# Loading the second chunk's last two units as 32x32 squares and transposing them on VectorE, in an HGRN2 and SwiGLU kernel

## The chip, the cores and the metric

The kernel runs on one core of a Trainium2 chip. The metric is device microseconds of one execution. The time before is the median of three runs; one more execution was recorded by the hardware profiler, and all times inside the kernel come from it.

## The reference

Four batches of eight heads, a sequence of 768 positions and a head size of 48 go through a gated linear attention. Its output is brought into 3072 rows of 384 features, which a SwiGLU feed-forward block (384 to 1536 to 384) takes.

```python
B, H, S, D = 4, 8, 768, 48
f = 1.0 / (1.0 + np.exp(-f_logit))
state = np.zeros((B, H, D, D))
for t in range(S):
    state = f[:, :, t, :, None] * state + einsum('bhd,bhe->bhde', k[:, :, t], v[:, :, t])
    y[:, :, t] = einsum('bhd,bhde->bhe', q[:, :, t], state)

x = y.transpose(0, 2, 1, 3).reshape(B * S, H * D)
g = x @ w_gate
out = (g * sigmoid(g) * (x @ w_val)) @ w_out
```

All inputs and the output are fp32.

## The kernel before

**Units and chunks.** The sequence is cut into six chunks of 128 positions. A unit is one chunk of one batch, numbered u = 4c + b, so that chunk 0 holds units 0 to 3, chunk 1 units 4 to 7, and so on. `attention(u)` is a generator that emits one unit in small steps. The feed-forward block works on a whole chunk of all four batches (512 rows) at a time, one chunk behind the attention. Chunk 0's feed-forward is `mlp_plain`: gate and value products (L786) and twelve down steps `downs_abreast` (L809). Chunks 1 to 5 use `mlp_fifteen`, a scheme with fifteen half-size products in place of eighteen (L988), made possible by sums of weights and of tokens that VectorE forms (L889, L892, L895), and seven down products in place of eight (L1087, L1150).

**What a unit does.** The gate logits f go through a sigmoid. f, k and q must stand with the features on partitions (head pairs, 48 of 64 rows each). Two scans along the positions give the running products of the gates (L601 into `tail`, L627 into `gate`). k is multiplied by one and q by the other (L559). The scores k q (`sc`, L647) are masked on VectorE (L662, tile `A`), the output y is formed from the masked scores and v, and from q and the decayed state (L683, L687 or L708), and the state is updated (`dS` L728, L737). `kt` (L651, L660) is k turned back for dS. The outputs go to `xT`, the input of the feed-forward block: for batches 0 to 2 through a copy `yT` and ten small DMAs each (L698), for batch 3 directly (L723). Batch 3 needs the decayed state laid out as a block diagonal for that (`diagonal`, L567 to L570); it uses the same one-buffer ring, tag "x", as `yT`.

**Two ways to turn f, k and q.** For chunks 0 and 1 (`c < SQUARES`, with SQUARES = 2) each of f, k and q is loaded by one DMA into one of two raw buffers (L444), in pieces of 48 values (192 bytes), and transposed by four TensorE transposes each (tiles fTp, kTp and qTp, L575). The sigmoid is taken while fTp leaves PSUM (L586), except for unit 4, whose sigmoid is taken ahead. For chunks 2 to 5 each is loaded by four DMAs (L440), in pieces of four positions of 48 values (768 bytes), into a tile of squares (`rooms`, one each for f, k and q, made by `make_rooms` when the first part's memory is given back). The sigmoid is taken in place (L580), and VectorE transposes 32x32 blocks (f: L589, k: L597, q: L631).

**What sets the order.** The kernel has two parts. In the second, from the load of unit 8 on, each engine's order is the order of emission; blocks of the feed-forward stage and steps of the attention are merged by a table of due times (`SCORES`, `CHAINS`, `times`), in units of the feed-forward's own nominal microseconds, where 0 is the start of a chunk's fifteen-product stage. The list `sigmoid` in `times` has the due time of each unit's sigmoid. In the first part `take_turns` emits the feed-forward pieces of chunk 0 and the attention steps of chunk 1 in proportion, and a scheduler of the framework may place an instruction earlier or later on its engine than it was emitted, when the operands of another are ready first. The attention steps of a unit come in four groups of 3, 6, 3 and 3 yields (`parts`), sorted so that group s of batch b has rank 2b + s. The sums of weights are emitted in pairs between the down steps and tied by `behind` to follow the VectorE instruction emitted last. Around units 6 and 7 the emission is: down step 0, scores of unit 6, down step 1, fTp of unit 7, down steps 2 and 3, y and dS of unit 6, down step 4, kTp and qTp of unit 7 with its scans and products, down step 5, scores of unit 7, down steps 6 and 7, y and dS of unit 7, down steps 8 to 11.

**Loads in the first part.** `load_after(u)` is called at the end of a unit's products. For units 4 and 5 it loads units 6 and 7, two units ahead, into the raw buffer that has come free.

**The end.** `judge` takes the least gate product of all units. Were it below 2^-60, a general path would run instead; a branch on it stands at the very end. A branch hint for all engines is given in the last stage.

The functions that the change touches:

Of the kernel before, what the change touches and what calls it, by code (L numbers as in the profile page):

```python
# [9 lines left out]
FP32 = mybir.dt.float32  # L10
# [280 lines left out]
def short_path(ctx, tc, ident, least, judge, q, k, v, f_logit, moe_w_gate, moe_w_val, moe_w_out, out):  # L291
# [9 lines left out]
    nc = tc.nc  # L301
    B, H, S, D = q.shape
    C = 128
    NCH = S // C
    HP = H // 2
    W = 64
# [6 lines left out]
    NRAW = 2  # L313
    NROT = 2
    NV = 4
    SQUARES = 2
# [3 lines left out]
    att = ctx.enter_context(tc.tile_pool(name="att", bufs=1))  # L320
# [5 lines left out]
    first_pool = early.enter_context(tc.tile_pool(name="first", bufs=1))  # L326
# [9 lines left out]
                            pattern=[[1, C]], channel_multiplier=-1)  # L336


    raw = {nm: [first_pool.tile([128, H, W], FP32, tag=f"{nm}raw{i}", name=f"{nm}raw{i}") for i in range(NRAW)]
           for nm in "qkf"}  # L340
    for nm in "fkq":
        for t in raw[nm]:
            nc.gpsimd.memset(t[:, :, D:W], 60.0 if nm == "f" else 0.0)
# [20 lines left out]
    def pairs(t, off=0):  # L364
        return t[:, off:off + HP * N1].rearrange("p (a t) -> p a t", t=N1)
# [23 lines left out]
    units = [(b, c) for c in range(NCH) for b in range(B)]  # L389
# [5 lines left out]
    Q = 32  # L395
    NI = C // Q
    RUN = NI * D

    rooms = {}

    def make_rooms(pool):
        for nm in "fkq":
# [22 lines left out]
    def load(u, what="fkqv"):  # L425
        b, c = units[u]
        rows = slice(c * C, (c + 1) * C)
        inputs = dict(f=f_logit, k=k, q=q, v=v)
        for nm in "fkqv" if c < SQUARES else "fqkv":
            src = inputs[nm]  # L430
            if nm not in what:
                continue
            if nm == "v":
                dst = v_of(u)
            elif c < SQUARES:
                dst = raw[nm][u % NRAW]
            else:
                for n in range(4):
                    at = Q * (1 - n % 2)
                    nc.sync.dma_start(  # L440
                        out=rooms[nm][Q * n:Q * (n + 1), at:at + HP * RUN].rearrange("t (a e) -> t a e", a=HP),
                        in_=src[b, n // 2::2, rows, :].rearrange("a (t i) d -> t a (i d)", i=NI))
                continue
            nc.sync.dma_start(out=dst[:, :, 0:D], in_=src[b, :, rows, :].rearrange("h t d -> t h d"))  # L444
# [100 lines left out]
    def attention(u):  # L545
        b, c = units[u]
# [2 lines left out]
        gate, tail = (x[u % NROT if c < SQUARES else 0] for x in (gates, tails))  # L549

        diagonal = None

        def multiply(out, x, by):

            if c >= SQUARES:
                for_each = "p a (t j i) -> p a t j i"
                out, by = (t.rearrange(for_each, j=2, i=NI // 2) for t in (out, by))
                x = x.rearrange("p (j a t i) -> p a t j i", j=2, a=HP, i=NI // 2)
            nc.vector.tensor_tensor(out, x, by, ALU.mult)  # L559

        def decay():
            nonlocal diagonal
            if c:
                nc.vector.tensor_tensor(decayed[:, :, 0:D], states[b], whole.broadcast_to((128, HP, D)), ALU.mult)
            if c and b == B - 1:

                diagonal = att.tile([128, HP, 2 * D], FP32, tag="x", name="diagonal")  # L567
                nc.scalar.copy(diagonal.rearrange("p a d -> p (a d)"), spare.broadcast_to((128, HP * 2 * D)))
                for par in range(2):
                    nc.scalar.copy(diagonal[rows_of(par), :, par * D:(par + 1) * D], decayed[rows_of(par), :, 0:D])  # L570

        def transposed(name, src):
            p = bank(name)
            for a in range(HP):
                nc.tensor.transpose(p[:, a * C:(a + 1) * C],  # L575
                                    src[:, 2 * a:2 * a + 2, :].rearrange("t r d -> t (r d)"), ident)
            return p.rearrange("p (a t) -> p a t", t=C)

        if c >= SQUARES:
            nc.scalar.activation(squares("f"), squares("f"), AF.Sigmoid)  # L580
            if b == (c > SQUARES):

                nc.scalar.activation(spare, spare, AF.Silu)
        else:
            p = transposed("fTp", fr)
            nc.scalar.activation(pairs(gate)[:, :, 1:N1], p, AF.Copy if u in ahead else AF.Sigmoid)  # L586
        yield
        if c >= SQUARES:
            nc.vector.transpose(in_turn(pairs(gate)[:, :, 1:N1]), squares("f"))  # L589
        yield  # L590

        kT = att.tile([128, HP, C], FP32, tag="kT", name="kT")
        qT = att.tile([128, HP, C], FP32, tag="qT", name="qT", bufs=2)
        kp, qp = kT, qT
        if c >= SQUARES:
            kp = qT.rearrange("p a t -> p (a t)")
            nc.vector.transpose(parted(kp), split_squares("k"))  # L597
        yield

        n = HP * N1  # L600
        nc.vector.tensor_tensor_scan(tail[:, 0:n][:, ::-1], gate[:, 0:n][:, ::-1], floor[:, ::-1], 1.0,  # L601
                                     op0=ALU.mult, op1=ALU.max)
        whole = pairs(tail)[:, :, 1:2]
        nc.vector.reciprocal(pairs(start)[:, :, 0:1], whole)
        yield
        if c < SQUARES:
            kp = transposed("kTp", kr)
            qp = transposed("qTp", qr)
        multiply(kT, kp, pairs(tail, 2)[:, :, 0:C])
        yield  # L610
        turned = SQUARES < c < NCH - 1
# [8 lines left out]
                                  in_=beside[Q * r:Q * (r + 1)].rearrange("t i (a e) -> t (i a) e", e=Q))  # L620
        yield

        if c >= SQUARES:

            nc.scalar.copy(least[:, u, :], whole.rearrange("p a t -> p (a t)"))
            whole = least[:, u, :].unsqueeze(2)
        nc.vector.tensor_tensor_scan(gate[:, 0:n], gate[:, 0:n], start, 1.0, op0=ALU.mult, op1=ALU.add)  # L627
        yield
        if c >= SQUARES:
            qp = tail[:, 0:HP * C]  # L630
            nc.vector.transpose(parted(qp), split_squares("q"))  # L631
            load_after(u)
        yield
        multiply(qT, qp, pairs(gate)[:, :, 1:N1])
        nc.gpsimd.memset(pairs(gate)[:, :, 0:1], 0.0)  # L635
        if 0 < c < SQUARES:
            load_after(u)
        if c < SQUARES:
            decay()
        yield  # L640
# [9 lines left out]
            for a in range(HP):  # L650
                nc.tensor.transpose(p[:, a * C:(a + 1) * C], kT[:, a, :], ident)  # L651
        yield
        if c < SQUARES:
            nc.scalar.copy(least[:, u, :], whole.rearrange("p a t -> p (a t)"))
        if c < NCH - 1:
            kt = att.tile([128, HP * C], FP32, tag="kt", name="kt")
# [82 lines left out]

    def load_after(u):  # L740

        w = u + (1 if units[u][1] >= SQUARES else 2)
        if w < len(units) and (units[w][1] >= SQUARES) == (w == u + 1):
            load(w, "fkqv" if units[w][1] < SQUARES or w == SQUARES * B else "fkq")

    def attention_steps(c):

        runs = [attention(c * B + b) for b in range(B)]
        parts = [3, 6, 3, 3]
        order = sorted((2 * b + s, b, n) for b in range(B) for s, n in enumerate(parts))  # L750
        return [lambda b=b, n=n: [next(runs[b]) for _ in range(n)] for _, b, n in order]

    traced = nc.cur_bb.bb.instructions
# [16 lines left out]
    TH = TB // 2  # L770
# [98 lines left out]
    def times(c):  # L869
        at = [t for t, _ in SCORES[c]]  # L870
        outputs = [*at[1:], down[10] if c + 1 in SCORES and SCORES[c + 1][0][0] < -1 else LAST]
        sigmoid = [-14 if c == 3 else SCORES[c - 1][-1][0] - whole - 0.01 if c > 3 else 0, -4 if c == 3 else at[0] - 0.01, *[t - 0.01 for t in at[1:]]]
        masks = {"b": 2, "o": 0.9, "A": 1.5}
        return [[f, *steps, s + 0.02, s + masks[kind], s + 2.2, o, o + 0.01, o + 2.1]
                for f, steps, (s, kind), o in zip(sigmoid, CHAINS[c], SCORES[c], outputs)]
# [404 lines left out]


    mark = traced[-1]
    waiting = []
    for c in range(2, NCH):
        for b in range(B):
# [34 lines left out]
@with_exitstack  # L1320
def kernel(
    ctx: ExitStack,
    tc: tile.TileContext,
    q: bass.AP,
    k: bass.AP,
    v: bass.AP,
    f_logit: bass.AP,
    moe_w_gate: bass.AP,
    moe_w_val: bass.AP,
    moe_w_out: bass.AP,  # L1330
    out: bass.AP,
):


    nc = tc.nc
    args = (q, k, v, f_logit, moe_w_gate, moe_w_val, moe_w_out, out)
    HP, D = q.shape[1] // 2, q.shape[3]
    flags = ctx.enter_context(tc.tile_pool(name="flags", bufs=1))
    least = flags.tile([128, q.shape[0] * q.shape[2] // 128, HP], FP32, tag="least", name="least")
    ident = flags.tile([128, 128], FP32, tag="idf", name="idf")  # L1340
    make_identity(nc, ident)
    redo = []

    def judge(bank):
        low = flags.tile([128, 1], FP32, tag="low", name="low")
        nc.vector.tensor_reduce(low, least, axis=mybir.AxisListType.XY, op=ALU.min)
        yield
        row = bank("row")[0:1, 0:128]
        nc.tensor.transpose(row, low, ident)
        one = flags.tile([1, 1], FP32, tag="one", name="one")  # L1350
        nc.vector.tensor_reduce(one, row.rearrange("p (n d) -> p n d", n=2)[:, :, 0:D], axis=mybir.AxisListType.XY, op=ALU.min)
        flag = flags.tile([1, 1], I32, tag="flag", name="flag")
        nc.vector.tensor_single_scalar(flag, one, LEAST, op=ALU.is_le)
        yield
        redo.append(nc.values_load(flag[0:1, 0:1], min_val=0, max_val=1,
                                   skip_runtime_bounds_check_because="a comparison"))
        tc.mark_branch_hint_location("redo", 0, list(nc.engines))
        yield

    short_path(tc, ident, least, judge, *args)  # L1360
    with tc.If(redo[0] > 0, label="redo"):
        general_path(tc, *args)
# [32 lines left out]
```

## Time and profile before

| | us |
|---|---|
| median of three runs | 608.66 (608.42 to 609.53) |
| the profiled execution | 609.78 |
| its span, first to last instruction | 608.0 |
| outside the span | 1.78 |
| PE busy | 592.7 (97%) |
| PE weight loads (overlap matmuls) | 487.8 (80%) |
| VectorE (DVE) busy | 476.9 (78%) |
| ScalarE (ACT) busy | 292.7 (48%) |
| GpSimd (POOL) busy | 70.1 (12%) |

Shares of busy time are means over the whole span. PE waits at times in the first 30 us; from there to 602.2 us it hardly pauses. PE instructions overlap, so the distance between their starts says more than their durations: a group of four transposes takes 0.44 us of the chain of waits, while one transpose is listed with 273 ns. The granted clock of TensorE is 0.999 over the run.

### The profile page before, as it was taken

Reading aid. Unit: us, or ns where it says so; the run is one execution under the profiler, and the core shown is the slowest. Engines: PE = TensorE matmul, PEld = TensorE weight load, DVE = VectorE, ACT = ScalarE, POOL = GpSimd, SP = SyncE. Lnnn points to the kernel's source line nnn. Section 1 sums busy time; section 2 is a strip of 40 time slices with the busy share of each in tenths; the row PEclk is TensorE's granted clock in tenths of the full one; section 3 lists DMA queues with packets and bytes.
Section 4 is the critical chain, followed back from the end, with each engine's and each line's share of the span. In section 5 each row is a group of like instructions: output and inputs, shape, how many; then the busy total and the mean of one; then the engine's idle time right before and its main releaser. Section 6 shows DMA issues by size and latency. Waiting matters only on the chain.

```text
span 608.0 us, 10812 instructions
## 1 busy us (share of the span) xinstructions
PE 592.7 (97%) x4028; PEld 487.8 (80%) x4028; DVE 476.9 (78%) x825; ACT 292.7 (48%) x557; POOL 70.1 (12%) x175
## 2 busy tenths in 40 slices
PE   7899999999999999999999999999999999999996
PEld 5744555667888899878899888898988899988896
DVE  7999885968999977988895978994878981666731
ACT  3567662314776512476622476732276731366600
POOL 1000000000030150030330030330030321000000
PEclk9999999999999999999999999999999999999999
DMA  9999461014331145333344333253241100100001
GB/s 202 236 246 357 140 196 27 8 33 130 79 92 48 37 113 129 93 96 96 77 111 122 91 101 95 62 135 85 74 105 52 28 8 8 53 1 1 1 1 56
DMA packets 110300, 55.12 MB, mean 91 GB/s; under 512 B 72992, under 2 KB 102688, under 8 KB 110240
## 3 DMA queue, kind: packets, MB, share of 16 engines
q1 hardware_dynamic: 103872, 47.67, 30.0%
q0 software_dynamic: 4352, 3.94, 2.0%
q10 hardware_dynamic: 2016, 2.75, 1.2%
q8 instruction: 33, 0.54, 0.4%
q14 instruction: 27, 0.22, 0.1%
HBM read 44.56 MB, written 6.82 MB: 85 GB/s over the span
## 4 chain that ended last, share of the span: by engine, by line
PE 84%; DVE 10%; DMA 2%; issue 1%; ACT 1%; POOL 1%; SPq 0%; ACTq 0%; DVEq 0%; POOLq 0%
PE o L1087 17%; PE A L988 15%; PE B L988 12%; PE gate L786 5%; PE val L786 5%; PE c L988 5%; PE o L988 5%; PE sc L647 4%; PE o L1150 3%; PE o L809 3%; PE y L708 2%; PE y L687 2%; PE dS L728 1%; PE y L683 1%; DVE c L892 1%
## 5 line engine op out<-in xcount | busy, mean ns | idle before, releaser
L698 POOL DMA_DIRECT2D xT<-yT x120 | 59.9, 507 | 53.8 <-ACT yT L691 52.2
L988 PE MATMUL A<-xs,w_both 128*128 128x256 f32 x240 | 62.3, 382 | 1.0 <-ACT c L993 1.0
L1087 PE MATMUL o<-w_out,h 128*128 128x192 f32 x360 | 62.0, 327 | 0.5 <-DVE h L940 0.5
L1087 PEld LDWEIGHTS o<-w_out,h 128*128 128x128 f32 x360 | 58.7, 190 | 1.7 <-DVE h L940 0.8
L993 ACT COPY c<-A 128x512 f32<-128x512 f32 x40 | 23.3, 582 | 58.9 <-PE A L988 48.9
L988 PEld LDWEIGHTS A<-xs,w_both 128*128 128x128 f32 x240 | 44.8, 190 | 7.9 <-ACT c L993 1.4
L993 ACT COPY aside<-A 128x512 f32<-128x512 f32 x60 | 35.0, 584 | 33.1 <-PE A L988 33.0
L889 DVE TENSOR_TENSOR c<-c,aside 128x512 f32<-128x512 f32 x60 | 41.1, 686 | 12.1 <-ACT aside L993 10.4
L940 DVE TENSOR_TENSOR h<-h,c 128x256 f32<-128x256 f32 x100 | 40.5, 414 | 7.8 <-ACT h L1004 7.6
L662 DVE TENSOR_TENSOR A<-sc,causal 128x512 f32<-128x512 f32 x48 | 30.9, 685 | 17.2 <-PE sc L647 17.1
L892 DVE TENSOR_TENSOR c<-c,aside 128x512 f32<-128x512 f32 x60 | 41.0, 683 | 2.5 <-ACT aside L993 2.5
L1004 ACT ACTIVATE h<-c 128x256 f32<-128x256 f32 x100 | 39.2, 416 | 7.8 <-DVE c L889 5.6
L1087 PE MATMUL o<-ws,h 128*128 128x192 f32 x240 | 41.5, 328 | 0.2 <-DVE A L662 0.2
L988 PE MATMUL B<-xs,w_both 128*128 128x256 f32 x160 | 41.3, 380 | 0.1
L988 PE MATMUL A<-xs,extra 128*128 128x256 f32 x160 | 41.3, 380 | 0.0
L988 PE MATMUL c<-xT,w_both 128*128 128x256 f32 x160 | 41.2, 380 | 0.1
L988 PE MATMUL B<-xT,extra 128*128 128x256 f32 x160 | 41.1, 379 | 0.0
L635 POOL MEMSET gates<- 128x4 f32 x24 | 2.9, 122 | 327.9 <-DVE qT L559 322.8
L993 ACT COPY aside<-B 128x512 f32<-128x512 f32 x60 | 35.1, 584 | 9.7 <-PE B L988 6.7
L1087 PEld LDWEIGHTS o<-ws,h 128*128 128x128 f32 x240 | 39.1, 190 | 0.8 <-DVE A L662 0.4
L889 DVE TENSOR_TENSOR c<-c,o 128x384 f32<-128x384 f32 x15 | 8.3, 552 | 36.8 <-PE o L1087 36.8
L892 DVE TENSOR_TENSOR c<-o,c 128x512 f32<-128x512 f32 x40 | 27.4, 684 | 10.6 <-ACT h L1004 6.2
(142 smaller groups left out, 1199.9 us busy)
## 6 DMA issues: line engine op xcount, KB each, us to landing
fsquares<-in_f_logit_dram SPq DMA_DIRECT2D x64, 96.0 KB, 2.5
qsquares<-in_q_dram SPq DMA_DIRECT2D x64, 96.0 KB, 2.2
ksquares<-in_k_dram SPq DMA_DIRECT2D x64, 96.0 KB, 2.3
v<-in_v_dram SPq DMA_DIRECT2D x24, 192.0 KB, 2.9
w<-in_moe_w_gate_dram SPq DMA_DIRECT2D x6, 768.0 KB, 6.5
w<-in_moe_w_val_dram SPq DMA_DIRECT2D x6, 768.0 KB, 5.4
w<-in_moe_w_out_dram SPq DMA_DIRECT2D x6, 768.0 KB, 4.6
out_dram<-ob ACTq DMA_DIRECT2D x14, 192.0 KB, 2.5
```

Source lines behind the costliest of these rows:

```text
L647: nc.tensor.matmul(sc[par][:, a * C:(a + 1) * C], lhsT=kT[r, a, :], rhs=qT[r, a, :], start=True, stop=True)
L662: nc.vector.tensor_tensor(A[:, par], sc[par].rearrange("p (a t) -> p a t", t=C), causal.unsqueeze(1).broadcast_to((128, HP, C)), ALU.mult)
L698: (nc.gpsimd if c >= SQUARES else nc.sync).dma_start(out=xT[c][f % 128:f % 128 + n, f // 128, b * C:(b + 1) * C], in_=yT[r:r + n, par, a / ...
L786: nc.tensor.matmul(p, lhsT=w[:, j, i, :], rhs=xT[c][:, i, :], start=(i == 0), stop=(i == KT - 1))
L809: nc.tensor.matmul(p, lhsT=hidden_tile(h, n // 2)[:, n % 2 * 2 + b // 2, b % 2 * C:(b % 2 + 1) * C], rhs=w_out[:, j, :], start=(n == 0), s ...
L889: nc.vector.tensor_tensor(dst, a, b, ALU.add)
L892: nc.vector.tensor_tensor(dst, a, b, ALU.subtract)
L940: lagging.append(lambda: f(*args))
L988: nc.tensor.matmul(p[name][:, n, :], lhsT=weights_of[a][:, n, j, :], rhs=tokens[b], start=fresh and n == 0, stop=True, skip_group_check=True)
L993: nc.scalar.copy(t, p[name])
L1004: nc.scalar.activation(dst, src[:, 0, :], AF.Silu)
L1087: nc.tensor.matmul(p[:, n, :], lhsT=lhsTs[j][:, n * C:(n + 1) * C], rhs=rhs[:, j, :], start=first and j == order[0] and n == 0, stop=j == ...
```

## The change

The function `by_squares(u)` is new: true for units 6 and 7 and for all of chunks 2 to 5. Units 6 and 7 are then loaded and transposed as the later chunks are. Their tile of squares is a view of 800 columns over both raw buffers of f, k or q, which become one tile for that; so unit 6 is loaded after unit 5's kTp and qTp have been read, and unit 7 after unit 6's q has been transposed. Their four DMAs each for f, k and q, and the one for v, are emitted in the order f, v, k, q. For these two units the attention groups are 1, 8, 3 and 3 yields, so that the VectorE transposes are emitted with the second group.

Three other edits come with it. In chunks 2 to 5 `diagonal` is taken from the ring "aside" of three buffers, which holds copies of products, and no longer from the ring of `yT`. The sigmoid of unit 13 (chunk 3, batch 1) is due at -1.5 instead of -4. The branch hint of SP is given at the start of the second part, those of the other engines where they were.

```diff
-    raw = {nm: [first_pool.tile([128, H, W], FP32, tag=f"{nm}raw{i}", name=f"{nm}raw{i}") for i in range(NRAW)]
-           for nm in "qkf"}
+    both_raw = {nm: first_pool.tile([128, NRAW, H, W], FP32, tag=f"{nm}raw", name=f"{nm}raw") for nm in "qkf"}
+    raw = {nm: [both_raw[nm][:, i] for i in range(NRAW)] for nm in "qkf"}
...
-    rooms = {}
+    rooms = {nm: t.rearrange("p n h w -> p (n h w)")[:, 0:Q + HP * RUN] for nm, t in both_raw.items()}
+
+    def by_squares(u):
+        return u >= SQUARES * B - 2
...
-        for nm in "fkqv" if c < SQUARES else "fqkv":
+        for nm in "fqkv" if c >= SQUARES else "fvkq" if by_squares(u) else "fkqv":
...
-            elif c < SQUARES:
+            elif not by_squares(u):
                 dst = raw[nm][u % NRAW]
...
-                diagonal = att.tile([128, HP, 2 * D], FP32, tag="x", name="diagonal")
+                if c < SQUARES:
+                    diagonal = att.tile([128, HP, 2 * D], FP32, tag="x", name="diagonal")
+                else:
+                    room = comb.tile([128, 2, TH], FP32, tag="aside", name="diagonal", bufs=3)
+                    diagonal = room.rearrange("p n t -> p (n t)")[:, 0:HP * 2 * D].rearrange("p (a d) -> p a d", a=HP)
...
-        if c >= SQUARES:
+        if in_squares:
             nc.scalar.activation(squares("f"), squares("f"), AF.Sigmoid)
-            if b == (c > SQUARES):
+            if c >= SQUARES and b == (c > SQUARES):
                 nc.scalar.activation(spare, spare, AF.Silu)
...
-        if c < SQUARES:
+        if not in_squares:
             kp = transposed("kTp", kr)
             qp = transposed("qTp", qr)
+            if by_squares(u + 1):
+                load(u + 1)
...
-        if 0 < c < SQUARES:
-            load_after(u)
...
-        w = u + (1 if units[u][1] >= SQUARES else 2)
-        if w < len(units) and (units[w][1] >= SQUARES) == (w == u + 1):
-            load(w, "fkqv" if units[w][1] < SQUARES or w == SQUARES * B else "fkq")
+        w = u + 1
+        if w < len(units) and w != SQUARES * B:
+            load(w, "fkqv" if units[w][1] < SQUARES else "fkq")
...
-        parts = [3, 6, 3, 3]
-        order = sorted((2 * b + s, b, n) for b in range(B) for s, n in enumerate(parts))
+        order = sorted((2 * b + s, b, n) for b in range(B)
+                       for s, n in enumerate((1, 8, 3, 3) if by_squares(c * B + b) else (3, 6, 3, 3)))
...
-        sigmoid = [-14 if c == 3 else SCORES[c - 1][-1][0] - whole - 0.01 if c > 3 else 0, -4 if c == 3 else at[0] - 0.01, *[t - 0.01 for t in at[1:]]]
+        sigmoid = [-14 if c == 3 else SCORES[c - 1][-1][0] - whole - 0.01 if c > 3 else 0, -1.5 if c == 3 else at[0] - 0.01, *[t - 0.01 for t in at[1:]]]
...
     mark = traced[-1]
+    tc.mark_branch_hint_location("redo", 0, [mybir.EngineType.SP])
...
-        tc.mark_branch_hint_location("redo", 0, list(nc.engines))
+        tc.mark_branch_hint_location("redo", 0, [e for e in nc.engines if e != mybir.EngineType.SP])
```

In the remaining places where the second way of turning f, k and q is chosen, `c >= SQUARES` becomes `in_squares`, which is `by_squares(u)`.

More of the change, by code (lines that the diff above doesn't have):

```diff
@@ L551, in attention @@
         diagonal = None
+        in_squares = by_squares(u)
         def multiply(out, x, by):
-            if c >= SQUARES:
+            if in_squares:
                 for_each = "p a (t j i) -> p a t j i"
@@ L577, in transposed @@
             return p.rearrange("p (a t) -> p a t", t=C)
-        if c >= SQUARES:
+        if in_squares:
             nc.scalar.activation(squares("f"), squares("f"), AF.Sigmoid)
-            if b == (c > SQUARES):
+            if c >= SQUARES and b == (c > SQUARES):
                 nc.scalar.activation(spare, spare, AF.Silu)
@@ L587, in attention @@
         yield
-        if c >= SQUARES:
+        if in_squares:
             nc.vector.transpose(in_turn(pairs(gate)[:, :, 1:N1]), squares("f"))
@@ L594, in attention @@
         kp, qp = kT, qT
-        if c >= SQUARES:
+        if in_squares:
             kp = qT.rearrange("p a t -> p (a t)")
@@ L621, in attention @@
         yield
-        if c >= SQUARES:
+        if in_squares:
             nc.scalar.copy(least[:, u, :], whole.rearrange("p a t -> p (a t)"))
@@ L628, in attention @@
         yield
-        if c >= SQUARES:
+        if in_squares:
             qp = tail[:, 0:HP * C]
@@ L652, in attention @@
         yield
-        if c < SQUARES:
+        if not in_squares:
             nc.scalar.copy(least[:, u, :], whole.rearrange("p a t -> p (a t)"))
```

## The prediction

> **What bounds the kernel now.** I read the page's busy table first, then busy time by stage, then the chain of waits through the second chunk's attention, then the list of PE's waits.
>
> ```profile
> span 608.0 us, 10812 instructions
> PE 592.7 (97%) x4028; PEld 487.8 (80%) x4028; DVE 476.9 (78%) x825; ACT 292.7 (48%) x557; POOL 70.1 (12%) x175
> ```
>
> PE is the only engine near the span. Busy matmul time may flatter, so I check with spacing: five of the six token chunks run through the fifteen-product stage, which begins at 144.28, 241.40, 337.38, 432.27 and 522.55 us and ends at 602.2. Sixty products of 0.86 us plus seven down products of 3.9 us are 78.9 us; the last stage, with no attention beside it, takes 79.65. PE is dense there, and work taken from PE comes off the span unless a new wait takes its place.
>
> The stretch that the change touches, units 6 and 7, in busy time by stage (columns: window, length, busy us of each engine with instruction counts, clock, DMA share, GB/s):
>
> ```profile
> 84.00:107.00 23.00, 23.00 (x122) 12.21 (x120) 13.99 (x24) 9.85 (x14) 0.10 (x1) 1.00 0.19 57
> 107.00:125.00 18.00, 17.73 (x115) 11.38 (x115) 17.69 (x29) 5.13 (x8) 0.10 (x1) 1.00 0.05 12
> 125.00:144.20 19.20, 19.20 (x139) 12.19 (x136) 13.35 (x26) 5.07 (x10) 0.24 (x3) 1.00 0.26 70
> ```
>
> VectorE has 9.0 us idle in the first window, 0.3 in the second, 5.85 in the third. The second is the danger: both engines are full. The chain of waits (start, us, piece) says the same:
>
> ```profile
> 84.51 0.44 PE fTp L575 x4
> ...
> 100.09 0.44 PE kTp L575 x4
> 100.53 0.44 PE qTp L575 x4
> ...
> 106.12 1.14 PE sc L647 x16
> 107.26 1.27 DVE A L662 x2
> ...
> 123.22 0.60 DVE kT L559
> 123.82 0.61 DVE qT L559
> ...
> 124.56 1.16 PE sc L647 x16
> ```
>
> From unit 6's scores (106.12) to unit 7's (124.56) the chain runs on VectorE. PE still had its own work nearly all that time; the list of PE's waits and that of ScalarE's (total, times, longest) give:
>
> ```profile
> PE sc L647 <- DVE qT L559: 2.6, 3, 1.5
> ...
> PE o L1087 <- ACT ob L1113: 1.3, 1, 1.3
> ```
>
> ```profile
> ACT diagonal L568 <- DMA xT<-yT: 35.5, 5, 10.6
> ```
>
> Of the 2.6 us only 0.28 falls at 124.56; the rest is in the first chunk. The 1.3 us is at 416.7, where ScalarE had stood 10.58 us before the diagonal copy of L568, and the output copy queued behind it.
>
> **What the Trainium skill says.** "Perfetto Trace Analysis", section Identifying the Most-Contended Engine, warns that matmul busy time is a poor measure and weight-load share a better one; the trace has 97% against 80%, which is why I take spacing. "VectorE: DVE Perf Modes", section The three transpose paths, says that VectorE turns independent 32x32 blocks while TensorE turns 128x128 into PSUM; it lists 311 against 390 ns for 128x128 in bf16. Here, in fp32, four tiles cost VectorE 0.70 us (k, q) or 1.11 us (f), and PE 0.44 us of chain. "DMA: Bandwidth & Descriptors", section Specifications, gives 512 B as the least transfer for full rate; raw loads move 192 B runs and land in 4.4 us, squares move 768 B runs and land in 2.5, which agrees. "Runtime: NRT & Kernel Launch", section Instruction fetch mechanics, says that a branch leaving the prefetched window waits for a fetch; PE's compare-and-branch took 1.97 us, SP's 0.07.
>
> **The change, part by part.**
> *Removed from PE:* for units 6 and 7 each the groups fTp, kTp, qTp, 0.44 us apiece: 6 x 0.44 = 2.64 us, all in a dense stretch.
> *Added to VectorE:* for each unit one f transpose, one k, one q, from these groups (busy us, mean ns):
>
> ```profile
> L589 DVE STREAM_TRANSPOSE gates<-fsquares 128x512 f32<-128x512 f32 x16 | 17.8, 1112 | 2.9 <-ACT fsquares L580 1.5 <-issue 1.3
> L597 DVE STREAM_TRANSPOSE qT<-ksquares 128x512 f32<-128x512 f32 x16 | 11.3, 704 | 0.0
> L631 DVE STREAM_TRANSPOSE tails<-qsquares 128x512 f32<-128x512 f32 x16 | 11.2, 699 | 0.9 <-ACT least L625 0.9
> ```
>
> 1.11 + 0.70 + 0.70 = 2.5 us a unit. The multiplications stay (kT<-qT 0.68 against kT<-kTp 0.68). Unit 6's 2.5 us lie in the 9.0 idle. Unit 7's decide. Its scores can start on PE at 124.28 - 2.64 = 121.64. VectorE starts unit 6's masks when PE gives scores, 1.3 us sooner: 107.25 - 1.3 = 105.95. From there to unit 7's qT it did 17.2 us (107.25 to 124.42). If all of it stays ahead, plus 2.5, qT is ready at 125.65. But two weight sums (121.93, 1.2 us) and two more (120.46, 1.2) stood ahead of kT only while it waited for kTp, which PE gave at 120.67; with k from VectorE that reason is gone. Unit 7's f needs no PE either, so its transpose (1.11) can fall in the idle 2.9 us before 107. Then qT is ready near 125.65 - 1.2 - 1.2 - 1.1 = 122.1, a wait of 0.4 us. Bounds: 0 to 4.0 us. I take 0.4, and the old 0.28 goes. Displaced sums go after unit 7's masks, where VectorE idled 4.8 us (129.0 to 133.8); token sums ended 2.6 us before the stage began, so that cover holds.
> *ScalarE:* sigmoid in place 0.63 against 0.60 from PSUM; same table loads: nothing, with half its time idle.
> *Loads:* each unit goes from 4 issues to 13 on SP, some 9 x 0.43 = 3.9 us more. Unit 6's set now waits for unit 5's transposes (72.5) and stands behind ten xT<-yT issues (69.08 to 75.7), so f lands near 75.7 + 1.7 + 2.5 = 80; its sigmoid ran at 91.07. Two w_out fetches (77.6) may slip by 5 us; their joins ran at 111 to 125. Unit 7's set can go when unit 6's f is turned (about 93) and xT<-yT of unit 5 is issued (99.8): f lands near 104, all by 108; its sigmoid ran at 112.2. Unit 6's own xT<-yT follow at 117.7, clear of it. Nothing, bound 0 to 1 us. One room instead of two raw buffers costs just this.
> *The diagonal in another ring, chunks 2 to 5:* removes 35.5 - 7.2 = 28.3 us of ScalarE waits, but only 1.3 us reached PE. Its new ring is used for copies of products, none of which run in the down stage; PE reads the diagonal at 233, 326, 421, 515, over 7 us before the next stage starts. Cost 0. The profiled run took 609.78 us (608.0 span, 1.78 around it), 1.12 over the median of 608.66, so the 1.3 us stall, after one slow transfer (6.0 us), may be peculiar to it: I take 0.4, bounds 0 and 1.3.
> *Sigmoid of unit 13, two half down products (3.9 us) later:* it waited 3.31 us for its load till 238.61; now it runs near 240, table load (1.28) and dummy (0.20) ending near 242.1, ahead of the copy at 242.29. Nothing; if 1 us late, the product's second bank covers it.
> *SP's branch hint at the start of the second part:* SP is idle 140.05 to 144.87 then; at the end its branch (603.0) stands ahead of waits for the last store (605.7). Even a 1.97 us fetch fits in 2.7. Nothing.
>
> Sum against the profiled execution: 609.78 - 2.64 - 0.28 + 0.4 - 1.3 = 605.96. Against the median: 608.66 - 2.64 - 0.28 + 0.4 - 0.4 = 605.7.
>
> **Rivals.** *VectorE eats the gain in part:* sums stay ahead of unit 7's chain, qT at 124.4, a wait of 2.8: 608.66 - 2.92 + 2.8 = 608.5. For it: 17.69 of 18 us busy. Against: 9.0 idle just before.
> *VectorE becomes the bound (slower):* nothing is hoisted, and the two sums traced next (125.20, 1.3 us) also slip in front, since they are ready at any time. qT at 125.65 + 1.3 = 126.95, scores 2.4 us later than now; 611.0. With the first half alone 609.8. It decides from the point where unit 7's scores start later than 125.8, 1.22 us past now.
> *Unit 7's loads queue behind unit 6's xT<-yT issues:* f lands near 126.5, scores near 134: 618. Against: those issues wait for unit 6's y at 117.
> *The transposes were hidden anyway:* that needs PE waiting there, and it waited 0.28.
>
> **Numbers.** Forecast 0.60, partial loss 0.16 (half of it still faster by over 0.2%), VectorE bound 0.17 (most slower), late loads 0.03, and 0.04 for a larger gain with 1.3 us from the ring. About 0.2%, 1.2 us, is what a measurement of this kernel can tell from no change. Faster 0.71, same 0.12, slower 0.17. Range: 608.66 - 2.92 - 1.3 = 604.4, with the scatter of 0.2, 604.2, up to 610.3, between the two prices of the slower rival.
>
> **What would show it.** No L575 groups for units 6 and 7 (24 of 96 PE transposes gone); L589, L597 and L631 at 18 each; unit 6's scores near 104.8, unit 7's near 122, the fifteen-product stage starting near 141.6 instead of 144.28, and later stages as long as now. The ring is right if L568 waits for xT<-yT only in chunk 1. I am wrong if unit 7's scores wait over 2 us for qT, or if ScalarE waits for a squares load before 110 us and PE behind it.

## The result and the profile after

The changed kernel takes **608.65 us** in the median of 22 runs (606.91 to 610.22), the kernel before 609.16 in 22 runs beside it (608.42 to 610.58). The ratio is 0.9984, with a 95% interval of 0.9977 to 0.9991: faster by 1.0 us, or 0.16% (the two medians lie 0.5 us apart; the ratio is used throughout). The forecast was 3 us. The sign was right and the size was a third, so most of the gain has to be looked for.

The profiled execution took 608.5 us, with a span of 606.7 (before: 609.78 and 608.0). The head of its page and the busy table:

```profile
span 606.7 us, 10798 instructions
PE 591.3 (97%) x4004; PEld 485.6 (80%) x4004; DVE 480.6 (79%) x831; ACT 295.1 (49%) x559; POOL 70.0 (12%) x175
```

PE has lost 24 instructions, the transposes of the six groups. But its busy time fell by only 1.4 us, less than the 2.64 us of chain that those groups took. Busy time by stage shows where (columns as before: window, length, busy us of PE, PEld, DVE, ACT and POOL with counts, clock, DMA share, GB/s):

```profile
84.00:107.00 23.00, 23.00 (x117) 11.92 (x116) 14.86 (x23) 7.42 (x11) 0.11 (x1) 1.00 0.38 118
107.00:125.00 18.00, 15.25 (x84) 9.02 (x83) 16.72 (x29) 5.10 (x8) 0.10 (x1) 0.91 0.23 66
125.00:143.50 18.50, 18.50 (x138) 11.62 (x137) 13.65 (x28) 5.67 (x9) 0.24 (x3) 1.00 0.26 69
```

In the second window PE is no longer full: 15.25 of 18.00 us, where it was 17.73. And the granted clock there is 0.91. In the last column but one, DMA traffic stands at 0.23 of the engines where it was 0.05: transfers have come into this window that used to be done before it. The list of PE's waits names the hole (total, times, longest):

```profile
PE o L817 <- DVE w_out L494: 2.7, 1, 2.7
PE sc L655 <- DVE qT L563: 2.4, 2, 1.6
```

The first line is new: the down product (`o`) waits 2.75 us for a join of `w_out`, a piece of the output weight, which arrives as 64-bit words and is put together as fp32 on ScalarE and VectorE. (The weights are 64-bit in memory: six fetches of 768 KB for 1536 x 384 values are 8 bytes a value.) The chain of waits leads back from there:

```profile
100.76 4.60 DMA w<-in_moe_w_out_dram
105.38 1.08 ACT up L481
...
113.44 0.88 DVE w_out L494
114.32 0.04 issue
114.36 4.51 PE o L817 x8
118.87 0.60 PE y L691 x16
...
126.30 1.09 PE sc L655 x16
...
145.94 0.86 PE A L996 x4
```

A fetch of `w_out` pieces that leaves at 100.76 passes through ScalarE and VectorE and reaches PE at 114.36. Eight down products then take 4.51 us (they take 2.6 to 2.85 where nothing is in the way), unit 7's scores start at 126.30, and the fifteen-product stage at 145.94, against 144.28 before. So this chunk **lost** 1.66 us where it should have gained 2.7, and the 1.3 us that the span gained came later: stage by stage between the starts of `A` products, nothing in chunk 1's (97.11 against 97.12), 0.67 in the next (95.31 against 95.98), 1.59 in the next (93.30 against 94.89), 0.02 in the next, and 0.64 from the start of the last stage to the end. -1.66 + 0.01 + 0.67 + 1.59 + 0.02 + 0.64 = 1.27.

Why does the fetch leave so late? SP is SyncE, the engine that issues these loads. Its timeline, first of the kernel before (start, us, issues), then of the one after:

```profile
75.81 0.53 SPq L461 DMA_DIRECT2D w<-in_moe_w_out_dram  x1
...
77.59 3.18 SPq L461 DMA_DIRECT2D w<-in_moe_w_out_dram  x2
```

```profile
87.00 1.74 SPq L443 DMA_DIRECT2D kraw<-in_k_dram  x4
89.19 0.79 SPq L443 DMA_DIRECT2D qraw<-in_q_dram  x2
93.39 6.22 SPq L706 DMA_DIRECT2D xT<-yT  x10
99.66 1.06 SPq L443 DMA_DIRECT2D qraw<-in_q_dram  x2
100.76 1.46 SPq L464 DMA_DIRECT2D w<-in_moe_w_out_dram  x3
```

The last three fetches of `w_out` used to leave at 75.81 and 77.59. Now they stand behind unit 7's loads, whose last two q squares stand behind the ten `xT` issues of unit 5, which wait until 93.39 for ScalarE to write `yT`. The traces show nothing that the fetch itself needs coming late: it leaves 0.04 us after the issue ahead of it. It slips by 23 to 25 us.

The queue is not the whole of the delay. The fourth join's own pieces were ready on VectorE at 108.41. Before it ran the join at 113.44, it ran masks (1.16 us), four sums of weights (2.40) and pieces of the next join (1.47).

### The profile page after: what moved, and what is told of

Same layout as the page of the kernel before. It is cut to its first block, busy times and chain, and to the rows that moved or that the text cites. A ratio compares the mean times of both kernels' runs of the same rounds, so it can differ in the third digit from the quotient of the medians.

```text
span 606.7 us, 10798 instructions
## 1 busy us (share of the span) xinstructions
PE 591.3 (97%) x4004; PEld 485.6 (80%) x4004; DVE 480.6 (79%) x831; ACT 295.1 (49%) x559; POOL 70.0 (12%) x175
## 3 DMA queue, kind: packets, MB, share of 16 engines
q10 hardware_dynamic: 2016, 2.75, 1.3%
## 4 chain that ended last, share of the span: by engine, by line
PE 75%; DVE 7%; issue 1%; ACT 1%; SPq 1%; DMA 1%; DVEq 0%; ACTq 0%
PE o L1095 19%; PE A L996 16%; PE B L996 13%; PE c L996 5%; PE o L996 5%; PE o L817 4%; PE o L1158 3%; PE sc L655 3%; PE y L695 2%; PE y L716 1%; PE y L691 1%; PE dS L736 1%; SPq L706 1%; DVE c L900 1%; DMA w<-in_moe_w_out_dram 1%
## 5 line engine op out<-in xcount | busy, mean ns | idle before, releaser
L817 PE MATMUL o<-w_out,h 128*128 128x384 f32 x96 | 33.9, 508 | 2.7 <-DVE w_out L494 2.7
```

The costliest lines, as they stand in the source:

```text
L817: nc.tensor.matmul(p, lhsT=hidden_tile(h, n // 2)[:, n % 2 * 2 + b // 2, b % 2 * C:(b % 2 + 1) * C], rhs=w_out[:, j, :], start=(n == 0), s ...
```

## The experiments

The theory, after this: **the squares give what was forecast, and the late `w_out` fetch takes it away**, partly by a wait of PE (TensorE) and partly by a lower TensorE clock behind the wait. The rivals: the squares give little because VectorE or the loads eat it (the forecast's own rivals), or the gain of 1 us is the three small edits' alone. All ratios are to the kernel before, run on the same chip.

**The fetch taken out of SP's queue**, in the kernel after (`b` is 1 for `w_out` pieces):

```diff
-    nc.sync.dma_start(out=kept["w"], in_=src)
+    (nc.sync if b > 1 else nc.gpsimd).dma_start(out=kept["w"], in_=src)
```

> The changed kernel with the six w_out fetches issued from GpSimd's queue, so that they no longer stand behind the squares' loads and the xT<-yT issues on SP. Late-fetch theory: the 2.75 us in which PE waited for the fourth w_out join (114.36 in the profile after) is gone, and with it the slow 4.51 us of the eight down matmuls behind it (2.6 us elsewhere): 608.65 - 2.75 - 1.9 = 604.0, ratio to before 0.9916, unit 7's scores near 122. VectorE theory: unit 7's qT stays at about 123.1 and PE waits for it instead: near 605.5, ratio 0.994, with 1.4 us or more of PE waiting for qT. If the fetch was not the cause: 608.6, ratio 0.999.

Measured: 604.31 against 609.48, ratio 0.9910 (0.9896 to 0.9925). The wait of `o` for `w_out` is gone from the list of PE's waits. From unit 6's scores to unit 7's it is 17.40 us (106.04 to 123.44 in the timeline), where the kernel after took 21.53 (104.70 to 126.23) and the one before 18.51. Between after and this, 0.9984 - 0.9910 = 0.74%, or 4.5 us, hang on the queue that these fetches stand in.

**The control: the same edit in the kernel before**, whose fetches were early anyway.

> The kernel before with the same move of the w_out fetches to GpSimd's queue. Late-fetch theory: nothing waits for them in the kernel before, so no change, 609.2, ratio 1.000 within 0.001. Rival, that the queue is better in itself (fewer issues on SP for any kernel): 1 us or more faster, ratio 0.998 or less.

Measured: 610.54, ratio 1.0018 (1.0008 to 1.0028). The queue itself brings no gain; it costs about 1 us, more than expected. In its profile PE waits 0.5 us for raw f in the first chunk, but the first gate product starts at 29.58, as in the kernel before (29.63), so that isn't the cost. The cause was not pursued. What matters here: the gain that the same edit brings in the kernel after is not a gift of GpSimd's queue.

**The three small edits**, together and singly, in the kernel before. The ring alone:

```diff
-                diagonal = att.tile([128, HP, 2 * D], FP32, tag="x", name="diagonal")
+                if c < SQUARES:
+                    diagonal = att.tile([128, HP, 2 * D], FP32, tag="x", name="diagonal")
+                else:
+                    room = comb.tile([128, 2, TH], FP32, tag="aside", name="diagonal", bufs=3)
...
```

> The kernel before with the diagonal of chunks 2 to 5 in the ring of copies, nothing else. If PE's wait of 1.3 us at 416.7 is in every execution: 609.4 - 1.4 = 608.0, ratio 0.9977, the stage from 337 us 1.6 us shorter (93.3 for 94.9). The forecast's size of 0.4: ratio 0.9993.

Measured: 608.39 against 609.43, ratio 0.9985 (0.9978 to 0.9993): about 0.9 us. The stage that it concerns took 93.30 us (338.46 to 431.76), as in every kernel with the ring, against 94.89 before and 93.81 to 94.23 in the three kernels without it that follow (hint, squares, sigmoid). PE's wait for ScalarE's output copy (`ob`) is in the list for all of these, with 0.2 to 1.3 us.

The branch hint alone:

```diff
     mark = traced[-1]
+    tc.mark_branch_hint_location("redo", 0, [mybir.EngineType.SP])
...
-        tc.mark_branch_hint_location("redo", 0, list(nc.engines))
+        tc.mark_branch_hint_location("redo", 0, [e for e in nc.engines if e != mybir.EngineType.SP])
```

> The kernel before with SP's branch hint early, nothing else. If the 2.7 us between SP's branch and its next instruction was a fetch: that gap falls to 0.5 to 1.0 us and the end comes 0.7 us sooner, when the last store has landed: 608.7, ratio 0.9988. The forecast (nothing): ratio 1.000.

Measured: 608.48 against 609.43, ratio 0.9982 (0.9975 to 0.9989): 1.1 us, where I had put nothing. SP's waits for itself say why, in the kernel before and with the hint (L1361 and L1362 are the branch's line):

```profile
SPq L1361 <- SPq L1361: 2.7, 1, 2.7
```

```profile
SPq L1362 <- SPq L1362: 2.0, 4, 0.7
```

Before, SP stood still for 2.7 us in one piece at its branch, from 603.0 to 605.7. With the hint it goes on 0.5 us after the branch (602.3 to 602.8), does most of its last waits early, and the longest pause is 0.7, until the last store has landed. From that landing to the end it is 2.3 to 2.8 us in the six profiles without the early hint and 1.7 to 2.2 in the six with it. That is some 0.6 us of the 1.1; the rest isn't accounted for.

The sigmoid alone (`-4` to `-1.5`):

> The kernel before with unit 13's sigmoid at -1.5, nothing else. Both the forecast and the comparison of stages say nothing: ratio 1.000, PE's wait of about 1.0 us near 262 still there. If the sigmoid is what took 0.7 us from the stage that begins at 241.4: ratio 0.9989 and that wait at 0.4.

Measured: 609.36 against 609.43, ratio 1.0003 (0.9993 to 1.0013): nothing, as forecast. In its list of PE's waits the wait of that stage is still there:

```profile
PE A L988 <- ACT c L993: 1.1, 1, 1.1
```

All three together:

> The kernel before with the three small edits alone (ring of the diagonal, sigmoid of unit 13 at -1.5, SP's branch hint early). From the two profiles: PE's wait of 1.3 us at 416.7 gone, 0.7 us of the wait near 262 gone, and 0.6 us less between the last store's issue and the end: 609.16 - 2.6 = 606.6, ratio 0.9957. The forecast's sizes (0.4 for the ring, nothing for the others): 608.8, ratio 0.9993.

Measured: 607.33 against 609.48, ratio 0.9962 (0.9947 to 0.9977). Within the intervals that is the sum of the three (-0.15, -0.18 and +0.03%). It is all that the kernel after has without its main change, and by the ratios it is **faster than the kernel after** (0.9984), though the two intervals meet at 0.9977. The squares, as they stand, give nothing, and may cost a little.

**The squares alone**, the kernel after without those three:

> The squares of units 6 and 7 alone: the ring of the diagonal, the sigmoid's due time and SP's branch hint as before. Late-fetch theory: the first part ends 1.66 us later than before (145.94 against 144.28) and nothing is won later: 610.8, ratio 1.0027, in the executions whose clock falls; 1.5 us less in those whose clock does not. Forecast's account, that the squares are the gain: 606.3, ratio 0.995.

Measured: 610.02 against 609.48, ratio 1.0004 (0.9995 to 1.0013): no gain, and less of a loss than the late fetch had been expected to cost (1.0027). One gain had not been reckoned with: the stage that starts at 243.8 us is 0.66 us shorter than before (95.32 against 95.98). Its profile repeats the story, with PE's wait of 2.4 us for `w_out`, and a fifteen-product stage that starts 116.02 us after the first gate product (30.70 to 146.72), where before it was 114.49 (29.63 to 144.12): 1.5 us lost.

**The clock behind the wait.** Finer windows of the kernel after, around PE's wait:

```profile
112.00:114.30 2.30, 0.00 (x0) 0.00 (x0) 2.30 (x5) 0.00 (x0) 0.00 (x0) 1.00 0.00 0
114.30:119.00 4.70, 4.64 (x16) 2.43 (x20) 3.70 (x8) 1.82 (x2) 0.00 (x0) 0.64 0.00 0
```

PE stands idle at full clock for the wait, and runs at 0.64 in the 4.7 us after it. More finely, the clock is at 0.50 for the 3.40 us from 114.30 to 117.70, and at 0.99 from there to 119. Half the clock for 3.40 us is a loss of 1.70. The rival: the eight records take 4.51 us because their weights come late in pieces, and the clock is a bystander. The experiment keeps PE busy through the wait with ten products on a constant, whose result nothing reads, ahead of the down step that waits:

```diff
+            if n == 3:
+                idle = bank("idle")
+                some = floor.bitcast(mybir.dt.bfloat16)
+                for _ in range(10):
+                    nc.tensor.matmul(idle, lhsT=some[:, 0:128], rhs=some[:, 0:512], start=True, stop=True)
```

> The changed kernel with ten matmuls on constants (their result is not used) ahead of the down step that waits for the late w_out join, so that PE is busy for about 2.2 of the 2.75 us. Clock theory, that the wait lets TensorE's clock fall and the next matmuls pay for it: the wait stays, but the eight matmuls behind it take 2.7 us and not 4.5, clock 0.999: 608.6 - 1.5 = 607.1, ratio 0.9963. If they are slow for another reason, or the filling gets in the way: 608.6 or more.

Measured: 607.49 against 609.43, ratio 0.9966 (0.9952 to 0.9979), 0.18% below the kernel after, with intervals that just touch. The same place in the timeline:

```profile
113.78 2.32 PE L838 MATMUL idle<-floor 128*128 128x512 bf16 x10
116.75 2.85 PE L817 MATMUL o<-w_out,h 128*128 128x384 f32 x8 [0.65 <-DVE w_out L494]
```

The join comes about as late as in the kernel after (this execution reached its first gate product 2.03 us later), PE still waits 0.65 us for it, and the eight records take 2.85 us instead of 4.51, at clock 1.00. From unit 6's scores to unit 7's it is 19.92 us instead of 21.53: adding useless work takes off 1.6 us. The weights come as late here, so the rival falls: the clock is the cause of that part. The scatter of the kernel after fits: of its 22 runs, 17 with a mean clock of 0.997 or less took 608.36 to 610.22 us, and five with 0.999 took 606.91 to 607.44. But a mean doesn't say where in a run the clock fell.

**Was the late weight needed at that step?** A row is here one of the twelve blocks of 128 features in `w_out`. The down step that waits is the fourth (n = 3). It reads row 7 of `w_out`. The join that it waits for is the fourth too, and that writes rows 3 and 9, which steps 6 and 7 read. Rows 3 and 9 are one slice with a stride of six, and row 7 lies between them. If the framework takes a strided slice for everything from its first row to its last, the wait is a false one. The experiment pairs neighbouring rows and takes them in turn, so that no join's rows enclose another's; each pair is still used at the same steps, with the hidden tiles that belong to it. SP's order stays as in the kernel after:

```diff
-        both = slice(i, NF, NF // 2)
+        both = slice(2 * i, 2 * i + 2)
...
-        j = n // 2 + n % 2 * NP
-        nc.tensor.matmul(p, lhsT=hidden_tile(h, n // 2)[:, n % 2 * 2 + b // 2, ...], rhs=w_out[:, j, :],
+        nc.tensor.matmul(p, lhsT=hidden_tile(h, n % NP)[:, n // NP * 2 + b // 2, ...], rhs=w_out[:, n, :],
```

> The changed kernel with w_out fetched and joined in pieces of two neighbouring rows (2i, 2i + 1) and the down steps taking rows 0 to 11 in turn; SP's queue is left in the same order, so the last three fetches are as late as in the changed kernel (about 100.8). Theory: down step 3 needed only rows that had been joined long before; it waited for the fourth join because that join's two rows (3 and 9) enclose row 7. With neighbouring rows nothing encloses anything: no wait at 114, clock kept, 608.65 - 2.75 - 1.9 = 604.0, ratio 0.991, as with the fetch moved. If down step 3 really needed the late data: the wait stays, 608.6, ratio 0.9985.

Measured: **604.46** against 609.28, ratio 0.9918 (0.9905 to 0.9932), the five runs within 0.4 us. The fetch is as late as in the kernel after, and PE doesn't wait. SP's timeline, PE's timeline and the chain of waits:

```profile
100.75 1.46 SPq L464 DMA_DIRECT2D w<-in_moe_w_out_dram  x3
```

```profile
106.32 7.91 PE L816 MATMUL o<-w_out,h 128*128 128x384 f32 x24
```

```profile
121.21 0.61 DVE qT L563
121.83 0.04 issue
121.87 1.16 PE sc L655 x16
...
141.58 0.86 PE A L995 x4
```

The fourth pair is still first read at steps 6 and 7, as in the kernel after. But VectorE's order has changed with the rows. The fourth join now starts here:

```profile
110.37 0.95 DVE L494 CUSTOM_DVE_ANT_0 w_out<-top,up 128x1536 uint16<-128x1536 uint16 x1
```

It ends at 111.32, just before the fourth step begins (the third group of eight in the 24, at about 111.5). So this run alone doesn't show that the step could have run without the join. That the tie was a false one follows from the code, where the step reads row 7 and the join writes rows 3 and 9, and from a wait the other way round in the kernel after. There the fifth join, of rows 4 and 10, waits 1.00 us for the same step:

```profile
118.91 0.96 DVE L494 CUSTOM_DVE_ANT_0 w_out<-top,up 128x1536 uint16<-128x1536 uint16 x1 [1.00 <-PE o L817]
```

No step has yet read rows 4 and 10, so nothing in the data asks for this wait. With neighbouring rows no join waits for PE. The same edit as a control in the kernel before:

> The kernel before with the same rows. PE did not wait for a join there: ratio 1.000 within 0.001. Rival, that the order of rows is worth something in itself: 0.998 or less.

Measured: 608.94 against 609.28, ratio 0.9996 (0.9988 to 1.0004). The order of rows is worth nothing in time where the fetches are early. Yet it moves the joins (before, then this run):

```profile
L491 DVE CUSTOM_DVE_ANT_0 w_out<-top,up x6: 932/952/959, 74.9 to 124.3; 128x1536 uint16<-128x1536 uint16 x6
```

```profile
L491 DVE CUSTOM_DVE_ANT_0 w_out<-top,up x6: 947/958/959, 75.4 to 101.1; 128x1536 uint16<-128x1536 uint16 x6
```

The last three joins start at 89, 98 and 101 us instead of 111, 118 and 124, though their fetches leave within 0.5 us of those before. So in the kernel before it was the order of rows, and not the fetches, that held these joins so late.

Both this version and the one with the other queue are 0.8 to 0.9% faster than the kernel before, and 0.7% faster than the kernel after. Between them the intervals don't decide.

## Why the prediction went wrong, step by step

**The step that failed is the one on the loads.** It saw the queue and the names: "Two w_out fetches (77.6) may slip by 5 us; their joins ran at 111 to 125", with "Nothing, bound 0 to 1 us" as its price. Three things in it were wrong.
- The slip: three fetches, and 23 to 25 us instead of 5. I had put unit 7's squares behind unit 5's `xT` issues, and with that "all by 108"; but I did not carry the same queue one place further, to the fetches that follow those loads.
- The slack: the joins' times were read as if they had room. In the kernel before the fourth join ended at 112.06 and the step tied to it began at about 113.2: the room was 1.2 us, and the tie itself, through the order of rows, wasn't seen. In the kernel after VectorE ended the fourth at 114.32, when the step was due at about 111.6 (114.36 less the 2.75 us).
- The price of a wait: I counted a wait of PE at its own length. The 2.75 us cost another 1.7 to 1.9 behind them, since eight records took 4.51 us instead of 2.6 to 2.85.

Together 4.6 us (2.75 + 1.85) against the -2.92 of the squares: +1.7, which is the measured +1.66 at the start of the fifteen-product stage. The 0.4 of waiting for qT does not come on top, since unit 7's scores come later than that here. The fetch on GpSimd's queue (0.9910) against the kernel after gives 4.5 by ratio.

One reading in that step was unsound as well, though no loss is traced to it. A raw transfer, which lands in 4.4 us, carries 192 KB, and one of the squares', which lands in 2.5 us, carries 96 KB, so the two times don't compare run lengths. And each set of squares is four transfers of 96 KB in place of one of 192: twice the bytes, which the forecast didn't count.

**PE's six groups and VectorE's 5 us: right.** With the false wait gone, unit 6's scores stand at 104.73 (forecast "near 104.8"), unit 7's at 121.87 with 0.21 us of waiting for qT (121.64 plus 0.4), the fifteen-product stage starts at 141.58 (141.6). Three terms of the sum, -2.64, -0.28 and +0.4, met to within 0.2 us. By ratios, the version with neighbouring rows against the three small edits alone is 0.9918 - 0.9962 = -0.44%, or -2.7 us, against -2.5 forecast. In the kernel after, too, PE has no wait from 78 us to this one at 112, and ScalarE none for a load of squares up to 130, so the loads of the squares themselves were in time. The slower rival, VectorE as the bound, fell: enough of the sums went behind unit 7's chain without a hand. (VectorE's other work did stand ahead of the fourth join in the kernel after, as said.) Its reversal point (unit 7's scores later than 125.8) was passed in the kernel after, at 126.3, but by the wait for `w_out`, not by unit 7's chain on VectorE.

**The diagonal's ring: right in kind, small by half.** -0.9 us with the ring alone, against -0.4, inside the bounds 0 to 1.3. That ScalarE waits for `xT` at L576 only once, in the second chunk, held:

```profile
ACT diagonal L576 <- DMA xT<-yT: 7.3, 1, 7.3
```

I had held that PE's stall in the profiled run might be peculiar to it; all six profiles without the ring show it, with 0.2 to 1.3 us.

**The sigmoid: nothing, right.**

**SP's hint: wrong, 0 for 1.1 us.** The forecast's "its branch (603.0) stands ahead of waits for the last store (605.7)" read a gap in SP's queue as a wait for the store. In that profile the store landed (605.67) just as the gap ended (605.73); with the ring alone it landed at 605.00, and SP went on only at 605.42. The gap was SP's own: the list of waits has it as SPq after SPq. "Runtime: NRT & Kernel Launch", section Instruction fetch mechanics of the Trainium skill, which the forecast used for PE, gives a possible reason, a fetch when a branch leaves the prefetched window. SP's 2.6 to 2.9 us from the branch to its next instruction without the early hint, against 0.5 to 1.1 with it, fit this; no trace here shows the fetch itself. Why the hint as it was given before, later in the program, did not serve is open.

**The clock.** "TensorE: Matmul & The Clock Gate", Part 1: The HAM clock gate, of the same skill says that an idle TensorE falls back to passing half its pulses after an idle window of about 3.4 us, and warns of waits for DMA in the middle of a kernel. The trace agrees on the half: the clock is at 0.50 for 3.40 us. The length of the idle does not quite agree: here 2.75 us of waiting was enough in the profiled run, and the mean clocks suggest the same of 17 of the 22. The page adds that its windows run freely, which fits that the clock seems to fall in some runs and not in others; this case doesn't show the windows themselves.

**What stays open.** The stage from 241 to 337 us is 0.7 us shorter in all kernels with squares for units 6 and 7 (95.31 to 95.34 against 95.91 to 96.34 without): PE's wait for ScalarE's copy there falls from 1.0 to 1.4 us to 0.4, the load of f for unit 14 landing 0.7 us sooner. It is not the sigmoid (the sigmoid alone and the three edits together have the wait), but why the load is sooner wasn't followed. The three small edits give 0.38% together in the kernel before, but 0.20% when they join the squares with the false wait (0.9984 against 1.0004); with intervals of some 0.15% on each ratio that is not read further. And the control on GpSimd's queue is 0.18% slower, as said.

## What to carry to other kernels

A load that is put on a queue can delay everything emitted after it on that queue by the wait of whatever it stands behind, as SP's did here, so follow the whole queue to its end, name what is next in it, and compare its new time with the **first consumer** in the list of waits, not with the time at which it used to be consumed. A wait on a busy TensorE can cost more than its length: 2.75 us cost another 1.7 here, because the clock fell. A few products that nobody reads can be cheaper than silence. And where an instruction waits for a write that it doesn't read, look whether the write is a strided slice that encloses it: neighbouring rows cost nothing and took 4 us off here. And before the time at which something ran is read as room, ask what held it there.

## What the runs showed of the hardware that I had not expected

- TensorE's granted clock fell to 0.50 for 3.40 us (a mean of 0.64 over 4.7) behind one wait of 2.75 us. In the one profile with ten unread products (2.32 us in all) it stayed at 1.00 there.
- From SP's branch to its next instruction at the end of the kernel it was 2.6 to 2.9 us in six profiles, and 0.5 to 1.1 us in six with the hint at the start of the second part; that edit alone made the kernel 0.18% faster.
- The same fetch on GpSimd's queue instead of SP's made the kernel before 0.18% slower (0.08 to 0.28%), and the kernel after 0.74% faster.
